# Attention of a fused RWKV-and-experts kernel listed as steps and ordered for every engine by a model, with the 64x64 tiles paired

## The chip, the cores and the metric

One core of a Trainium2 chip. The metric is the device time of one execution in microseconds, the median of the runs shown; a profile is one further execution. TensorE is the matrix engine, VectorE, ScalarE and GpSimd the elementwise engines, SyncE (SP) issues most DMAs.

## The reference

Inputs r, k, v, w, a, b have shape (4, 8, 768, 40): 4 batches, 8 heads, 768 steps, 40 dimensions, float32. Attention is a recurrence over time with a 40x40 state per batch and head; its output, reshaped to 3072 rows of 320, goes through a mixture of 8 experts, one expert per row.

```python
for t in range(S):
    y[:, :, t] = np.einsum('bhd,bhde->bhe', rt, state)
    Sa = np.einsum('bhde,bhe->bhd', state, at)
    state_decay = state * wt[:, :, None, :] - np.einsum('bhd,bhe->bhde', Sa, bt)
    state = state_decay + np.einsum('bhd,bhe->bhde', vt, kt)
...
logits = x @ w_gate
expert_idx = np.argmax(logits, axis=1)
...
h = np.maximum(x_sorted[lo:hi] @ w1[e], 0.0)
y_sorted[lo:hi] = h @ w2[e]
...
return gate_w[:, None] * y
```

## The kernel before

Attention works on 24 units: a unit is one chunk of 64 time steps for two batches, which makes 16 heads in 4 groups p of four. Units alternate between the two pairs of batches (bh), so unit u needs the state of unit u-2. Within a chunk the recurrence becomes products of 64x64 blocks and the inverse of a triangular matrix, taken by repeated squaring (X, X squared and so on) with TT collecting the product of the terms M = 1 + X.

A block takes a quarter of TensorE's 128x128 array: rows 0-63 or 64-127 for the operands, columns 0-63 or 64-127 for the result. `TILES` (L166) walks the four quarters, first the two on the diagonal, then the two that cross. Each fp32 matmul shows in the trace as two matmul and two weight-load records.

- `load(u)` (L196) issues eight DMAs on SP: four of the decays (`dec`, L204) and four of the five other inputs (`in`, L205).
- `prepare(u)` (L207) runs two scans on VectorE (L212, L217), scales K, B and A on GpSimd (L222 to L224), and transposes V, K and B in twelve 128x128 transposes (L230), copied by ScalarE (L235).
- `systems` (L242) forms N (L254), T1 (L267) and G (L284), the product gv (L296), and the inverse: squares (L312), copied by ScalarE (L319, L322), plus one on GpSimd in two halves (`plus_one`, L276), times TT (L329), copied by VectorE (L334).
- `attend` applies the state: ST (L350), r (L354), rhs (L358), u (L363), S (L377), the first part of y (L384), uT (L393), ZT (L407), the new state st (L420, L426) and the rest of y (L440, L448); xT is written at L453. The groups gv, u, S and the first y name the same half for operands and result, so they use the two diagonal quarters only.
- `route` (L458) forms the gate's logits (L466), transposes xT (L470), takes a softmax weight and stores the rows to `x_rows` (L482).

The loop at the end of attention calls load(u+3), prepare(u+2), systems(u+1), attend(u) and route(u); the tile framework orders the instructions from that listing, with `tc.issue_after` (L400, L445) moving two groups behind others. All PSUM results come from one pool of four tiles of two banks (`bank2`, L190). At the start GpSimd clears the padding of the four input buffers in eight halves (L181) and of the other buffers (L184 to L188), and the weights of the first two experts are fetched (`fetch`, L154) ahead of the loop. After attention one core-wide routing step counts and sorts the rows (L507 to L605), and the experts run: gather by indirect DMA (L615), transposes (L625), layer one (L634), layer two (L647), indirect store (L653).

## Time and profile before

| what | us |
|---|---|
| median of 3 runs | 1298.59 |
| runs | 1302.38, 1289.19, 1298.59 |
| the profiled execution's own time | 1284.12 |
| its span, first to last instruction | 1282.4 |
| TensorE matmul busy in the span | 1007.2 (79%), 24316 records |
| TensorE weight loads | 761.6 (59%), 24316 records |
| VectorE, ScalarE, GpSimd | 370.2, 252.2, 406.2 |
| mean granted TensorE clock | 0.896 of full speed |

Busy time is the union of an engine's instructions; matmuls overlap and their ends are modelled, so a busy TensorE is not one at its peak. [...] "Idle before" is the time an engine stood still ahead of an instruction, with what released it behind the arrow; "issue" means that it waited for nothing that the profile shows.

### The profile page before, as it was taken

To read this page: it belongs to the slowest core of one execution; us is meant where nothing else is said; L and a number is where in the kernel's file an instruction comes from. 1 tells how busy PE (TensorE), PEld (TensorE's weight loads), DVE (VectorE), ACT (ScalarE), POOL (GpSimd) and SP (SyncE) were. 2 spreads that over 40 slices of the span, in tenths; PEclk is the share of its full clock that TensorE was granted. 3 is DMA by queue.
4 is the path that set the end of the run, shared out by engine and by line. 5 is a ranking of instruction groups with operands and counts; after the bars stand their busy time and mean duration, and the time that the engine had idled before them with its cause. 6 is when DMAs were issued, how large, how long until landed. Compare 5 with 4: busy or idle time off the path is not lost. (4 is left out here: it accounts for less than half of the span.)

```text
span 1282.4 us, 51696 instructions
## 1 busy us (share of the span) xinstructions
PE 1007.2 (79%) x24316; PEld 761.6 (59%) x24316; DVE 370.2 (29%) x694; ACT 252.2 (20%) x519; POOL 406.2 (32%) x497
## 2 busy tenths in 40 slices
PE   0677777778777777777777877777399999999997
PEld 0566667767666667767666766666235544554444
DVE  0434333333333333333433333331521111011100
ACT  0222222222222222222222222222000011010010
POOL 9643333333333332333333323222332210210011
PEclk9979898887978897887988789889689999999998
DMA  5601112211211121210111111000023322321100
GB/s 155 138 4 44 36 39 40 39 39 22 39 26 34 39 40 39 39 37 19 39 33 33 39 39 35 8 9 9 23 76 109 115 72 74 91 97 52 48 15 16
DMA packets 112682, 61.02 MB, mean 48 GB/s; under 512 B 96849, under 2 KB 108115, under 8 KB 112468
## 3 DMA queue, kind: packets, MB, share of 16 engines
q1 hardware_dynamic: 109056, 48.51, 15.7%
q0 software_dynamic: 3072, 9.18, 2.4%
q8 instruction: 191, 3.13, 1.0%
q14 instruction: 23, 0.19, 0.0%
q10 hardware_dynamic: 340, 0.01, 0.0%
HBM read 49.82 MB, written 9.18 MB: 46 GB/s over the span
## 5 line engine op out<-in xcount | busy, mean ns | idle before, releaser
L276 POOL TENSOR_TENSOR M<-X,ihalf 128x256 f32<-128x256 f32 x240 | 188.7, 809 | 116.9 <-ACT X L322 103.3
L312 PE MATMUL ps_sq<-X 64*64 64x64 f32 x6912 | 175.8, 231 | 35.4 <-ACT X L322 33.1
L634 PE MATMUL hp<-xgT,w 128*128 128x512 f32 (+1 forms) x384 | 192.1, 630 | 0.0
L329 PE MATMUL ps_TT<-TT,M 64*64 64x64 f32 x3840 | 122.8, 240 | 73.1 <-POOL M L276 52.5
L312 PEld LDWEIGHTS ps_sq<-X 64*64 64x64 f32 x6912 | 146.1, 143 | 52.1 <-ACT X L322 47.7
L334 DVE COPY TT<-ps_TT 128x512 f32<-128x512 f32 x120 | 82.9, 691 | 274.5 <-PE ps_TT L329 270.3
L329 PEld LDWEIGHTS ps_TT<-TT,M 64*64 64x64 f32 x3840 | 97.2, 150 | 93.0 <-POOL M L276 89.3
L647 PE MATMUL zp<-w,h_sb 128*128 128x320 f32 x512 | 145.1, 433 | 0.0
L634 PEld LDWEIGHTS hp<-xgT,w 128*128 128x128 f32 (+1 forms) x384 | 63.4, 189 | 123.4 <-issue 122.3
L322 ACT COPY X<-ps_sq 128x512 f32<-128x512 f32 x192 | 103.1, 589 | 141.4 <-PE ps_sq L312 140.1
L224 POOL TENSOR_TENSOR in<-in,q 128x512 f32<-128x512 f32 x24 | 29.3, 1220 | 294.8 <-DVE q L217 294.8
L647 PEld LDWEIGHTS zp<-w,h_sb 128*128 128x128 f32 x512 | 94.6, 191 | 34.5 <-issue 0.8
L639 DVE TENSOR_SCALAR h_sb<-hp 128x512 f32<-128x512 f32 x32 | 22.1, 692 | 247.3 <-PE hp L634 247.3
L653 POOL DMA_INDIRECT out_dram<-zo,s_idx x32 | 31.7, 989 | 181.4 <-ACT zo L652 180.2
L230 PE MATMUL ps_nat<-ident,in 128*128 128x128 f32 x288 | 50.6, 322 | 39.4 <-DMA in<-in_packed_dram 21.2
L276 POOL TENSOR_TENSOR TT<-T,ihalf 128x256 f32<-128x256 f32 x48 | 33.8, 725 | 126.8 <-DVE T L271 126.8
L412 DVE TENSOR_TENSOR ZT<-ps_ZT,m_nn 128x512 f32<-128x512 f32 x24 | 16.6, 691 | 176.0 <-PE ps_ZT L407 176.0
L615 POOL DMA_INDIRECT xg<-x_rows,g_idx x32 | 30.7, 960 | 109.1 <-PE tp L625 78.9
L230 PEld LDWEIGHTS ps_nat<-ident,in 128*128 128x128 f32 x288 | 38.9, 165 | 44.0 <-issue 21.5
L641 ACT ACTIVATE h_sb<-hp 128x512 f32<-128x512 f32 x32 | 19.1, 597 | 198.5 <-PE hp L634 198.5
L296 PE MATMUL ps_gv<-natV,G 64*64 64x40 f32 x768 | 32.3, 229 | 23.3 <-DVE G L289 23.2
L363 PE MATMUL ps_u<-rhs,TT 64*64 64x40 f32 x768 | 36.6, 264 | 17.9 <-DVE rhs L358 17.9
(156 smaller groups left out, 1256.9 us busy)
## 6 DMA issues: line engine op xcount, KB each, us to landing
in<-in_packed_dram SPq DMA_DIRECT2D x96, 200.0 KB
w<-in_moe_w_dram SPq DMA_DIRECT2D x8, 1280.0 KB
w<-in_moe_w_dram SPq DMA_DIRECT2D x8, 1024.0 KB
dec<-in_packed_dram SPq DMA_DIRECT2D x96, 40.0 KB
x_rows<-xs SPq DMA_DIRECT2D x48, 80.0 KB
w<-in_moe_w_dram SPq DMA_DIRECT2D x8, 256.0 KB
xg<-x_rows,g_idx POOLq DMA_INDIRECT x32, 3.0
out_dram<-zo,s_idx POOLq DMA_INDIRECT x32, 2.5
```

Source lines behind the costliest of these rows:

```text
L230: nc.tensor.transpose(ps[:, i % 2, p * 128 : (p + 1) * 128], I[:, n, 2 * p : 2 * p + 2, :].rearrange("x q t -> x (q t)"), ident[:],)
L276: nc.gpsimd.tensor_tensor(dst, src, eye[:, : NP, :], op=ALU.add)
L296: nc.tensor.matmul(gv[halves[q], par, p, :], lhsT=G[halves[q], par, 0, p, :], rhs=Vn[halves[q], p, par, :D], start=True, stop=True,)
L312: nc.tensor.matmul(ps[halves[s], h, w, p, :], lhsT=X[halves[h], s, 1 - w, p, :], rhs=X[halves[h], s, w, p, :], start=True, stop=True,)
L322: nc.scalar.copy(Y[:, s], ps[:, s])
L329: nc.tensor.matmul(ps[halves[s], h, 0, p, :], lhsT=Mk[halves[h], s, p, :], rhs=TT[halves[h], s, p, :], start=True, stop=True,)
L334: nc.vector.tensor_copy(TT[:], ps[:, :, 0])
L363: nc.tensor.matmul(pu[halves[q], par, p, :], lhsT=TT[halves[q], par, p, :], rhs=rhs[halves[q], par, p, :D], start=True, stop=True,)
L615: nc.gpsimd.indirect_dma_start(out=g["xg"][:, j, :], out_offset=None, in_=x_d[:, :], in_offset=bass.IndirectOffsetOnAxis(ap=g["gi"](j), ax ...
L634: nc.tensor.matmul(hp[:, :cols], lhsT=g["w"][0][:dsz, db, fb * 128 : (fb + 1) * 128], rhs=g["xT"][:dsz, db, :cols], start=(db == 0), stop= ...
L647: nc.tensor.matmul(zp[:], lhsT=g["h"][:, fb, j * 128 : (j + 1) * 128], rhs=g["w"][1][:, fb, :], start=(fb == 0), stop=(fb == FB - 1),)
L653: ins_ = nc.gpsimd.indirect_dma_start(out=out[:, :], out_offset=bass.IndirectOffsetOnAxis(ap=g["si"](j), axis=0), in_=zo[:], in_offset=Non ...
```

## The change

Attention is no longer run as functions called unit by unit. `unit(u)` lists steps: each `Step` has an engine, a duration in us (a round of four tiles is `ROUND = 0.116`), a function that emits its instructions, and the buffers that it reads and writes (`Held`). `in_order()` then places all steps of all 24 units by a greedy list: of the steps whose inputs are there in the model, the one that can start earliest on its engine is emitted next, ties by rank (the unit's number, the preparation one unit and the loads three units ahead). Steps marked ANY (PSUM copies) go to ScalarE or VectorE, whichever starts earlier. PSUM is one tile of eight banks, and a step's result gets one or two banks when it is placed. Inside `tc.manual_schedule` every engine runs its instructions in this order.

The layout changes too: N is written crosswise (`halves[1 - q]`), so that TT, gv, u and uT use crossing tiles where they used diagonal ones. gv is interleaved with S, and u with the first part of y. T1's own 16 products are gone; T1 is taken from X by `plus_one` and moved between the halves by four products with `ihalf`, 256 columns wide. GpSimd adds the identity in one instruction instead of two halves, and the last M is added by VectorE. The gate's logits and the transpose of xT are one product with `turn_gate` (the identity beside the negated gate weights). Clearing is shared between GpSimd and VectorE, and the first two experts' weights are fetched in the middle of attention. The experts and the routing step are not touched.

The core of the diff (the functions from `bank2` to the loop over units are removed; only what replaces them is shown):

```diff
-    wg_sb = rte.tile([128, NP, E], F32)
-    nc.gpsimd.memset(wg_sb[:], 0.0)
+    turn_gate = rte.tile([128, NP, 128 + E], F32)
+    nc.gpsimd.memset(turn_gate[:, :, 128:], 0.0)
     for par in range(2):
         nc.scalar.dma_start(
-            wg_sb[par * HP : par * HP + D], moe_w_gate.rearrange("(p a e) n -> a e p n", a=2, e=D)[par],
+            turn_gate[par * HP : par * HP + D, :, 128:], moe_w_gate.rearrange("(p a e) n -> a e p n", a=2, e=D)[par],
         )
+    nc.gpsimd.tensor_scalar(turn_gate[:, :, 128:], turn_gate[:, :, 128:], scalar1=-1.0, scalar2=None, op0=ALU.mult)
+    nc.gpsimd.tensor_copy(turn_gate[:, :, :128], ident[:, None, :].to_broadcast([128, NP, 128]))
...
+    class Step:
+        def __init__(self, rank, eng, cost, fn, reads=(), writes=(), after=(), lag=0.2):
+            self.rank, self.eng, self.cost, self.fn, self.lag = (rank, len(steps)), eng, cost, fn, lag
+            self.deps, self.done, self.next, self.ps = set(after), 0.0, [], []
...
+            steps.append(self)
...
+    def in_order():
+        free = {e: 0.0 for e in (PE, DVE, ACT, POOL, SP)}
+        bank_free = [0.0] * 8
...
+        def place(new, t):
+            ok = [f is not None and f <= t for f in bank_free]
+            at = []
+            for h in new:
+                n = h.banks
+                b = next((b for b in (range(7, -1, -1) if n == 1 else range(7)) if all(ok[b : b + n])), None)
+                if b is None:
+                    return None
+                ok[b : b + n] = [False] * n
+                at.append(b)
+            return at
+        for s in steps:
+            for d in s.deps:
+                d.next.append(s)
+        ready = {s: 0.0 for s in steps if not s.deps}
+        while ready:
+            times = sorted({f for f in bank_free if f is not None})
+            best = None
+            for s, r in ready.items():
+                new = [h for h in s.ps if h.at is None]
+                for e in ((ACT, DVE) if s.eng == ANY else (s.eng,)):
+                    t0 = max(r, free[e])
+                    if best is not None and t0 > best[0][0]:
+                        continue
+                    at = ()
+                    if new:
+                        for t in [t0] + [x for x in times if x > t0]:
+                            at = place(new, t)
+                            if at is not None:
+                                break
+                        else:
+                            continue
+                        t0 = t
+                    cost = s.cost * (1.17 if s.eng == ANY and e == DVE else 1.0)
+                    key = (t0, s.rank, t0 + cost)
+                    if best is None or key < best[0]:
+                        best = (key, s, e, t0, cost, new, at)
+            _, s, e, t, cost, new, at = best
+            del ready[s]
+            for h, b in zip(new, at):
+                h.at = b
+                bank_free[b : b + h.banks] = [None] * h.banks
+            free[e] = t + cost
+            s.done = t + cost + s.lag
+            s.fn(e)
+            for h in s.ps:
+                h.users -= 1
+                if h.users == 0:
+                    for b in range(h.at, h.at + h.banks):
+                        bank_free[b] = s.done
+            for n in s.next:
+                waits[n] -= 1
+                if waits[n] == 0:
+                    ready[n] = max(d.done for d in n.deps)
...
+    ROUND = 0.116
...
+        psum = pp.tile([128, 8, 512], F32, name="ps")
...
+        r_in = Ring("in", [5, SEG, C], 4, 5)
+        r_dec = Ring("dec", [SEG * C1 + 1], 2)
...
+        r_X = Ring("X", [2, 2, NP, C], 5, 2)
+        r_M = Ring("M", [2, NP, C], 3)
+        r_TT = Ring("TT", [2, NP, C], 4)
+        r_G = Ring("G", [2, 2, NP, C], 2, 2)
...
+        for i, (t, held) in enumerate(r_in.bufs):
             for lo in (32, 96):
...
+                zero(-99 + 5 * i, POOL if lo == 32 else DVE, 1.2, t[lo : lo + 32], held)
+        for t, held in r_qini.bufs:
+            zero(-98, POOL, 0.6, t[:], held)
+        for r in (r_rhs, r_ST, r_S):
+            for t, held in r.bufs:
+                zero(-50, POOL, 0.6, t[:], held)
...
+            Step(u - 3, SP, 1.7, lambda e: load(e, 0), writes=hdec, lag=2.5)
+            Step(u - 3, SP, 1.7, lambda e: load(e, 1), writes=hI, lag=3.5)
...
+            def plus_one(x, hx, w):
+                m, hm = r_M.take()
+                Step(u, POOL, 1.25, lambda e: nc.gpsimd.tensor_tensor(m[:], x[:, :, w], eye, op=ALU.add), reads=hx, writes=hm)
+                return m, hm
+            def times(stat, mov, reads, ps):
+                def fn(e):
+                    t = pair(ps, C)
                     for p in range(NP):
                         for h, s in TILES:
...
+                            mm(t[halves[s], h, p, :], stat(h, s, p), mov(h, s, p))
+                Step(u, PE, 4 * ROUND, fn, reads=reads, writes=[ps])
+            def new_TT(ps):
+                t, ht = r_TT.take()
+                Step(u, ANY, 0.59, lambda e: copy(e, t[:], pair(ps, C)), reads=[ps], writes=ht)
+                return t, ht
+            T1, hT1 = plus_one(X, hX, 1)
+            ps = Held(2)
+            def moved(e, ps=ps):
+                t = pair(ps, C)
+                for h, s in TILES:
+                    mm(t[halves[s], h].rearrange("x p j -> x (p j)"), ihalf[halves[h]], T1[halves[h], s].rearrange("x p j -> x (p j)"))
+            Step(u, PE, 4 * ROUND, moved, reads=hT1, writes=[ps])
+            TT, hTT = new_TT(ps)
...
...
+                    Step(u, PE, 8 * ROUND, squares, reads=hX, writes=[ps])
+                    X, hX = r_X.take()
+                    for s in range(2):
+                        Step(u, ANY, 0.59, lambda e, s=s, ps=ps, X=X: copy(e, X[:, s], whole(ps)[:, s]),
+                             reads=[ps], writes=hX[s : s + 1])
+                    M, hM = plus_one(X, hX, 0)
+                else:
+                    times(lambda h, s, p, X=X: X[halves[h], s, 1, p, :], lambda h, s, p, X=X: X[halves[h], s, 0, p, :], hX, ps)
+                    M, hM = r_M.take()
+                    Step(u, DVE, 0.69, lambda e, ps=ps, M=M: nc.vector.tensor_tensor(M[:], pair(ps, C), eye, op=ALU.add),
+                         reads=[ps], writes=hM)
+                ps = Held(2)
+                times(lambda h, s, p, M=M: M[halves[h], s, p, :], lambda h, s, p, TT=TT: TT[halves[h], s, p, :], hM + hTT, ps)
+                TT, hTT = new_TT(ps)
...
+            def p_gv(e):
+                for p in range(NP):
+                    for i in range(2):
+                        for q in range(2):
+                            par = q ^ i
+                            mm(single(psg)[halves[1 - q], par, p, :], G[halves[q], par, 0, p, :], nV[halves[q], p, par, :D])
+                        if c:
+                            for par in range(2):
+                                mm(single(psS)[halves[par], i, p, :], ST[halves[par], i, p, :], ihalf[halves[par], :D])
+            Step(u, PE, 8 * ROUND, p_gv, reads=hG + hnV + (hST if c else []), writes=[psg] + ([psS] if c else []))
...
+            def p_u(e):
+                t = single(psu)
+                for p in range(NP):
+                    for i in range(2):
+                        for q in range(2):
+                            par = q ^ i
+                            mm(t[halves[q], par, p, :], TT[halves[1 - q], par, p, :], rhs[halves[1 - q], par, p, :D])
+                        if c:
+                            for par in range(2):
+                                mm(
+                                    pair(psy, C)[halves[par], i, p, :], Sn[halves[par], i, p, :], head(R, p, i, par),
+                                    start=(p == 0), stop=False,
+                                )
+            s_u = Step(u, PE, 8 * ROUND, p_u, reads=hTT + hrhs + (hSn + [hI[R]] if c else []), writes=[psu] + ([psy] if c else []))
...
+            Step(u, PE, 4 * ROUND, p_uT, reads=hTT + hrhs, writes=[ps], after=[s_u])
...
+            late = u + 1
+            s_ = bh * NCH + c
+            psx = Held(2)
+            WX = 128 + E
+            def p_x(e):
                 for p in range(NP):
...
+                    mm(psum[:, psx.at + p // 2, p % 2 * WX : (p % 2 + 1) * WX], xT[:, p].rearrange("x q j -> x (q j)"), turn_gate[:, p, :])
+            Step(late, PE, 0.95, p_x, reads=hxT, writes=[psx])
...
+        for u in range(NU):
+            unit(u)
+        def first_weights(e):
+            for i in range(2):
+                weights[i] = fetch(moe_w1[i], moe_w2[i])
+        Step(8, SP, 2.0, first_weights, after=[s for s in steps if s.eng == SP][-3 * (NU - 12) - 1 :][:1])
+        with tc.manual_schedule(engines={getattr(mybir.EngineType, n) for n in ENGINES}):
+            in_order()
```

## Rows read from the trace of the kernel before

**Rows 1.** Busy time by stage: columns length, busy time (instructions) per engine, granted clock, DMA share, GB/s.
```profile
44.00:905.00 861.00, 654.25 (x23271) 587.73 (x23271) 302.00 (x512) 214.42 (x446) 297.76 (x354) 0.87 0.16 33
905.00:1282.00 377.00, 346.80 (x1024) 169.39 (x1022) 61.33 (x176) 33.62 (x67) 67.66 (x68) 0.95 0.21 67
```

**Rows 2.** Line L453 on VectorE, the write of xT: all 24, and the last but one.
```profile
L453 DVE TENSOR_TENSOR xT<-ps_y,q x24: 690/691/692, 98.5 to 903.1; 128x512 f32<-128x512 f32 x24
...
889.21 0.69 DVE L453 TENSOR_TENSOR xT<-ps_y,q 128x512 f32<-128x512 f32 x1 [1.28 <-PE ps_y L448]
```

**Rows 3.** Groups by line: busy us, mean ns; idle before and its releasers.
```profile
L276 POOL TENSOR_TENSOR M<-X,ihalf 128x256 f32<-128x256 f32 x240 | 188.7, 809 | 116.9 <-ACT X L322 103.3 <-ACT X L319 13.4
...
L329 PE MATMUL ps_TT<-TT,M 64*64 64x64 f32 x3840 | 122.8, 240 | 73.1 <-POOL M L276 52.5 <-DVE TT L334 18.6 <-issue 0.8
L322 ACT COPY X<-ps_sq 128x512 f32<-128x512 f32 x192 | 103.1, 589 | 141.4 <-PE ps_sq L312 140.1 <-POOL M L276 1.3
...
L334 DVE COPY TT<-ps_TT 128x512 f32<-128x512 f32 x120 | 82.9, 691 | 274.5 <-PE ps_TT L329 270.3 <-POOL M L276 4.3
...
L212 DVE TENSOR_TENSOR_SCAN rv<-dec,ones 128x521 f32<-128x521 f32 x24 | 38.6, 1609 | 33.0 <-DMA dec<-in_packed_dram 32.4 <-DMA in<-in_packed_dram 0.6
...
L222 POOL TENSOR_TENSOR in<-in,rv 128x512 f32<-128x512 f32 x24 | 29.3, 1220 | 0.8 <-DVE rv L212 0.8
```

**Rows 4.** Timeline of TensorE, 450 to 459 us and at 757.75: start, length, records.
```profile
451.21 1.13 PE L363 MATMUL ps_u<-rhs,TT 64*64 64x40 f32 x32 [0.85 <-DVE rhs L358]
452.14 1.18 PE L377 MATMUL ps_S<-ihalf,ST 64*64 64x40 f32 x32
...
456.68 0.63 PE L420 MATMUL ps_st<-natV,natK 64*64 64x40 f32 x32
457.12 0.66 PE L426 MATMUL ps_st<-U,natB 64*64 64x40 f32 x32
...
757.75 0.66 PE L230 MATMUL ps_nat<-ident,in 128*128 128x128 f32 x4
```

**Rows 5.** DMA queues of the page: packets, MB, share of 16 engines.
```profile
q8 instruction: 191, 3.13, 1.0%
```

**Rows 6.** Timeline of TensorE, 818.7 to 822.6 us, the first and the last of six rows.
```profile
818.79 0.33 PE L407 MATMUL ps_ZT<-in,uT 64*64 64x64 f32 x9
...
822.18 0.34 PE L448 MATMUL ps_y<-G,natK 64*64 64x64 f32 x8 [1.20 <-issue]
```

**Rows 7.** Timeline of TensorE, 872 to 877 us, the rows after two stalls.
```profile
872.52 0.50 PE L312 MATMUL ps_sq<-X 64*64 64x64 f32 x18 [0.15 <-issue]
...
876.22 0.50 PE L329 MATMUL ps_TT<-TT,M 64*64 64x64 f32 x18 [0.46 <-issue]
```

**Rows 8.** Slices of 0.2 us, columns as in rows 1.
```profile
819.40:819.60 0.20, 0.20 (x28) 0.20 (x22) 0.20 (x1) 0.00 (x0) 0.00 (x0) 1.00 0.37 82
870.00:870.20 0.20, 0.20 (x30) 0.20 (x21) 0.00 (x0) 0.00 (x0) 0.00 (x0) 1.00 0.29 82
873.60:873.80 0.20, 0.03 (x1) 0.03 (x1) 0.20 (x1) 0.20 (x2) 0.00 (x0) 1.00 0.38 82
```

**Rows 9.** TensorE after two stalls while inputs load, and a slice between them.
```profile
761.22 0.35 PE L284 MATMUL ps_G<-in 64*64 64x64 f32 x8 [0.21 <-issue]
...
767.24 1.44 PE L312 MATMUL ps_sq<-X 64*64 64x64 f32 x42 [0.33 <-issue]
...
763.50:764.00 0.50, 0.50 (x34) 0.50 (x32) 0.00 (x0) 0.00 (x0) 0.00 (x0) 1.00 0.87 116
```

**Rows 10.** The start: the first 32 us by engine, GpSimd's clears, the first scan, the first N.
```profile
0.00:32.00 32.00, 1.09 (x4) 0.71 (x4) 0.00 (x0) 1.87 (x2) 30.28 (x68) 1.00 0.58 155
...
14.73 11.27 POOL L181 MEMSET in<- 32x2560 f32 x5
...
32.35 1.24 DVE L212 TENSOR_TENSOR_SCAN rv<-dec,ones 128x521 f32<-128x521 f32 x1 [32.35 <-DMA dec<-in_packed_dram]
...
44.14 1.99 PE L254 MATMUL ps_N<-in 64*64 64x64 f32 x64
```

## Prediction

> **What bounds the kernel now.** I read the page's busy shares first, then busy time by stage, the groups of instructions, one unit's timeline, and last the DMA traffic in slices of 0.2 us. The stages [rows 1]: attention runs from 44 to 905 us (861 us for 24 units), routing and experts from 905 to 1282, which the diff leaves alone. In attention TensorE is busy 654 of 861 us at a mean granted clock of 0.87, VectorE 302, GpSimd 298, ScalarE 214: no engine is full. The output step ends at 98.5 us for the first unit and 903.1 us for the last [rows 2], 35 us apart on average. Inside a unit the engines hand one chain back and forth: TensorE's products for TT waited 73 us, mostly for GpSimd's M, GpSimd 103 us for ScalarE's X, ScalarE 140 us for TensorE's squares, VectorE 270 us for TT's products [rows 3]. So the order binds first: the systems of unit u+1 run almost alone, then attend(u) almost alone. That is what the change goes after.

> **Pairing.** Four groups of 16 matmuls (u, S, the first y, gv) use only the two diagonal tiles. From L363's start to L377's: 0.93 us for 32 records (16 fp32 matmuls, two records each); the products of L420, on all four tiles, take 0.44 [rows 4]. Paired, gv with S and u with the first y, each group loses 0.49 us: 4 x 0.49 x 24 = 47 us of TensorE time, on the path as long as TensorE sets the pace. T1's 16 products give way to 4 wide ones with ihalf (256 columns each, four times a usual one's; an estimate, 0.46 us in place of 0.46, so nothing).

> **Order.** If it does what it lists, the fullest engine sets the pace. TensorE per unit: 464 ordinary matmuls are 116 rounds of four, the wide ones 4 more; a round is 0.44/4 = 0.11 to 0.116 us, 13.8 us. 12 transposes at 0.66 us per four at most [rows 4] are 1.65 to 2.0; the gate products, four where there were twelve instructions, 0.5 to 1.4, I take 0.95. Sum 16.5 us. VectorE and ScalarE: some 25 PSUM reads of 512 columns at 0.69 or 0.59 us, two scans of up to 1.6 [rows 3], and some 5 us (an estimate by size) of six reads of 320 columns and of small ones: 24 us over two engines, 12 each. GpSimd: three multiplies at 1.22 and five additions of 512 columns, bounded by one and two of today's halves (0.81 to 1.62 [rows 3]), nearer to the multiply of the same size: 3.7 + 5 x 1.4 = 10.7. A bank pair is held from its first matmul to its last read, 1.4 to 4 us, psy 6: some 90 bank-us per unit, 11.5 us over 8 banks. All lie under TensorE's 16.5, which lies under today's 35. By engines alone a unit could come at 17.7 (with drains between tile modes) to 20 us.

> [...]

> After the change a unit has 468 matmuls x 2 + 8 + 12 = 956 records and as many weight loads, against 984: 24 units less the first and last chunks' savings make 22,624 x 2 / 256 = 176.8 blocks. So 176.8 x 3.7 = 654 us is the least, however good the order. Loads delay a fetch: at 767.24 a block came 6.0 us after the stall at 761.22, with the DMA engines 0.87 busy at 763.5 us in between [rows 9]. Loads keep them so for about 6.5 us of each unit; I charge one or two blocks of 7.4 with 1 to 2 us more, 0.3 us on the mean, and bound it by 0 and 2.3. Where the granted clock falls to half, a block's 16 rounds need 3.7 us themselves and only waits add. I take 4.0 us a block, between 3.6 and 4.4: 707 us, 29.5 per unit. In that state the pairing's 47 us and most of the order's gain lie under the fetch; they are worth something only down to this floor.

> **Start, weights, tail.** Today the two experts' weights go first on SP, the first scan waits for dec until 32.35 us, GpSimd clears input buffers, eight halves at 2.25 us, until 26 us, and the first N product starts at 44.14 [rows 10]; the DMA moved 155 GB/s meanwhile. The change defers the weights and gives half the clearing to VectorE: GpSimd has 26 - 8 x 2.25 = 8 us of constants, then four halves, 9 us, some 4 us of smaller clears (an estimate by size) and two multiplies, 2.4: N at 23 to 28 us, I take 25; at worst 44. The 5.1 MB of weights then lie inside attention: 33 us at 155 GB/s, in which blocks take 6.0 instead of 4.0: 10 us (0 to 15). Behind the fetch on SP's queue wait the next units' loads, which have two units' lead and hide. The last unit has nobody to fill its waits: today the last attend takes 13.9 us alone, from one xT to the next [rows 2]; I add 12 (5 to 20).

> **The sum.** Attention's end: 25 + 707 + 10 + 12 = 754 us, against 905: 151 less. The profiled execution took 1284.1 us (span 1282.4), so 1133 us. The runs shown have a median of 1298.6, 1.1% above that execution; I keep 1133.

> **Rivals.**
> (a) The supply does not bind: the stalls are chance, or fetches run further ahead in a dense stream. For it: only 8 us of stalls today. Against it: blocks average 4.74 us today, so a deeper store would always be full, yet it ran dry after one block. Then units at 19 us: 25 + 456 + 12 = 493, 412 less: 872 us.
> (b) The order does not hold: each engine's list is fixed, and where a duration is off (GpSimd beside VectorE's scans, a cold clock), the engine stands at its head with ready work behind. For it: the durations in the list are constants, and it has 1.25 us for an addition whose two halves take 1.62 today [rows 3]. Against it: waits then must cover all the slack between 16.5 and 30 us. A block every 4.5 us: 796 + 47 = 843, 62 less: 1222 us.
> (c) Slower: fetches collide with loads all the time, since a faster PE also asks for loads sooner, and every block takes 6.0 us as at 767.24: 1061 + 47 = 1108, 203 more: 1487 us. It decides from (905 - 47)/176.8 = 4.85 us per block. Against it: a unit's loads fill only 6.5 us of its time, and no faster than units end.

> **How the numbers follow.** Forecast 0.72, (a) 0.14, (b) 0.09, (c) 0.05. The forecast's own range, 3.6 to 4.4 us per block with the start and tail bounds, is 1055 to 1205. I give 1045 to 1210: it leaves out (a), most of (c) and the far part of (b). A difference of about 1% is what a measurement of this kernel can tell from none; faster by more than that 0.94 (forecast, (a), most of (b)), within it 0.02, slower 0.04.

> **What would show it.** Right: attention ends near 754 us; no engine is full, TensorE about 55 to 65% busy there; its idle time stands under "issue", not under semaphores, in stalls of 1 to 2 us about every 254 instructions; single 16.4 KB bursts come every 3.6 to 4.0 us where nothing else is loaded; the diagonal groups' 0.93 us are gone; N starts at about 25 us. Wrong: units at 17 to 20 us with blocks under 2.5 us (a); TensorE waiting mostly for ScalarE, VectorE or GpSimd (b); blocks over 4.85 us (c).

## The result, and the profile after

The changed kernel takes 1103.14 us (median of 4 runs, 1101.03 to 1109.93) against 1297.48 for the kernel before (a fourth run of it took 1296.37): a ratio of 0.852 (95% interval 0.846 to 0.858), 194 us less. The forecast was 1133, with a range of 1045 to 1210. The profiled execution took 1102.44 us with a span of 1100.7. Medians and ratios below leave out slow runs, those over 1.5% above the fastest of the same kernel: one of the first merge (1076.04 us) and two of the kernel before.

The page of the changed kernel, busy times, clock, and the DMA queue that carries instructions:

```profile
PE 837.7 (76%) x23644; PEld 614.6 (56%) x23644; DVE 400.8 (36%) x769; ACT 247.5 (22%) x504; POOL 340.1 (31%) x318
...
PEclk9999899899989979998999899957999999999998
...
q8 instruction: 186, 3.05, 1.2%
```

The write of xT, which ends attention (it answers to [rows 2]), and busy time by stage (to [rows 1]; the columns are length, busy time of TensorE, weight loads, VectorE, ScalarE and GpSimd with their instructions, granted clock, DMA share, GB/s):

```profile
L637 DVE TENSOR_TENSOR xT<-ps,q x24: 680/692/693, 76.0 to 716.6; 128x512 f32<-128x512 f32 x24
```

```profile
30.40:390.00 359.60, 253.42 (x11937) 230.76 (x11937) 174.17 (x307) 114.90 (x235) 140.18 (x106) 0.95 0.23 45
390.00:411.00 21.00, 13.12 (x459) 11.43 (x461) 7.04 (x13) 3.12 (x6) 1.27 (x1) 0.76 1.01 272
411.00:685.00 274.00, 195.76 (x9171) 177.91 (x9170) 130.21 (x233) 82.41 (x172) 98.75 (x75) 0.94 0.19 38
685.00:716.60 31.60, 21.99 (x1056) 19.62 (x1046) 10.48 (x20) 9.90 (x20) 5.07 (x4) 0.98 0.04 10
716.00:1100.70 384.70, 349.08 (x1052) 171.36 (x1044) 62.73 (x178) 33.54 (x67) 67.77 (x68) 0.94 0.22 66
```

All of the gain lies in attention: the last xT comes at 716.6 us instead of 903.1, 186.5 earlier, 28 us apart on the mean instead of 35. What follows is 4.8 us longer (384.1 after 379.3 us, from the last xT to the end of the span).

Is TensorE's time the limit now? No: it is busy in 484 of attention's 686 us. The groups by line and the waits on TensorE say what it does in the rest:

```profile
L358 PE MATMUL ps<-X 64*64 64x64 f32 x6912 | 148.1, 228 | 68.3 <-issue 67.0 <-ACT TT L353 1.2
...
L358 PE MATMUL ps<-TT,M 64*64 64x64 f32 x3840 | 94.9, 228 | 37.2 <-issue 36.7
```

```profile
PE ps L358 <- issue: 193.7, 149, 4.5
...
PE ps L358 <- ACT TT L353: 2.4, 6, 0.7
PE ps L358 <- DVE ZT L621: 0.9, 1, 0.9
```

Before, the products for TT stood idle 73 us, most of it for GpSimd's M and VectorE's TT [rows 3]. Now they stand idle 37 us, nearly all of it for nothing that the profile names. So do all of TensorE's products: 194 us in 149 stalls (the columns of the waits are us in total, times, longest). The timeline of TensorE shows where these stalls are. Start, length, records, and in brackets the idle time before; all rows between the first two stalls, and the rows at the next two:

```profile
43.31 0.28 PE L358 MATMUL ps<-TT,M 64*64 64x64 f32 x4 [2.07 <-issue]
43.41 0.22 PE L358 MATMUL ps<-X 64*64 64x64 f32 x1
43.42 0.23 PE L358 MATMUL ps<-TT,M 64*64 64x64 f32 x3
43.47 1.11 PE L358 MATMUL ps<-X 64*64 64x64 f32 x63
44.51 0.66 PE L411 MATMUL ps<-ident,in 128*128 128x128 f32 x4
45.10 1.03 PE L358 MATMUL ps<-X 64*64 64x64 f32 x52
47.19 0.39 PE L358 MATMUL ps<-X 64*64 64x64 f32 x11 [1.06 <-issue]
...
50.75 0.37 PE L358 MATMUL ps<-natV,G 64*64 64x40 f32 x6 [1.14 <-issue]
...
54.57 0.45 PE L358 MATMUL ps<-X 64*64 64x64 f32 x13 [1.63 <-issue]
```

Count the records between the first two brackets: 4 + 1 + 3 + 63 + 4 + 52 = 127, with as many weight loads 254 instructions. The next stall comes 128 records on, the next 127. The line of the program and the kind of product don't matter; the count does. This is the block of about 256 instructions that [rows 6, 7] showed now and then (the first bare section below has 128 records to the block, 256 instructions with their weight loads), and here most blocks end so: counted over all records of attention, there are 141 stalls of over 0.3 us under "issue" for some 176 blocks, and each lies a whole number of blocks behind the one before, to within two records: one block 113 times, two 21 times, three 6 times. A single block takes 3.80 us in the median (3.45 at the least), whereas the products between 43.31 and 47.19 keep TensorE busy for under 3.

And where nothing else is loaded, slices of 0.2 us show the block's transfer itself, as in [rows 8]:

```profile
644.80:645.00 0.20, 0.20 (x29) 0.20 (x24) 0.04 (x1) 0.00 (x0) 0.00 (x0) 1.00 0.33 82
648.40:648.60 0.20, 0.20 (x21) 0.18 (x13) 0.20 (x1) 0.20 (x1) 0.00 (x0) 1.00 0.30 82
652.20:652.40 0.20, 0.20 (x27) 0.20 (x23) 0.00 (x0) 0.00 (x0) 0.00 (x0) 1.00 0.30 82
655.80:656.00 0.20, 0.20 (x10) 0.15 (x3) 0.00 (x0) 0.03 (x1) 0.20 (x1) 1.00 0.43 82
```

One burst every 3.6 to 3.8 us, 16.4 KB each (82 GB/s over 0.2 us). The packets of the instruction queue, taken one by one from the trace, tie burst and stall together: in each of the 113 single blocks exactly one packet of 16,384 bytes starts, 1.17 us after the block was entered in the median (1.04 to 5.49), and TensorE goes on 2.16 to 2.89 us after that start. So where a block comes late, it is mostly because its packet started late.

### The profile page after: what moved, and what is told of

Its sections match the earlier page's. It is cut to its first block, busy times and chain, and to the rows that moved or that the text cites. A ratio compares the mean times of both kernels' runs of the same rounds, so it can differ in the third digit from the quotient of the medians.

```text
span 1100.7 us, 50357 instructions
## 1 busy us (share of the span) xinstructions
PE 837.7 (76%) x23644; PEld 614.6 (56%) x23644; DVE 400.8 (36%) x769; ACT 247.5 (22%) x504; POOL 340.1 (31%) x318
## 5 line engine op out<-in xcount | busy, mean ns | idle before, releaser
L442 POOL TENSOR_TENSOR M<-X,ihalf 128x512 f32<-128x512 f32 x120 | 165.0, 1378 | 349.3 <-DVE X L355 194.0
L358 PE MATMUL ps<-X 64*64 64x64 f32 x6912 | 148.1, 228 | 68.3 <-issue 67.0
L358 PEld LDWEIGHTS ps<-X 64*64 64x64 f32 x6912 | 131.1, 142 | 79.2 <-issue 75.7
L358 PE MATMUL ps<-TT,M 64*64 64x64 f32 x3840 | 94.9, 228 | 37.2 <-issue 36.7
L353 ACT COPY TT<-ps 128x512 f32<-128x512 f32 x122 | 71.6, 587 | 193.5 <-PE ps L358 187.0
L358 PEld LDWEIGHTS ps<-TT,M 64*64 64x64 f32 x3840 | 79.5, 141 | 45.2 <-issue 43.2
L353 ACT COPY X<-ps 128x512 f32<-128x512 f32 x109 | 62.8, 587 | 172.0 <-PE ps L358 170.0
L355 DVE COPY X<-ps 128x512 f32<-128x512 f32 x83 | 57.3, 690 | 107.6 <-PE ps L358 106.2
L358 PE MATMUL ps<-in 64*64 64x64 f32 x3072 | 61.6, 223 | 23.8 <-issue 23.5
L401 POOL TENSOR_TENSOR in<-in,rv 128x512 f32<-128x512 f32 x48 | 60.8, 1276 | 47.5 <-DMA in<-in_packed_dram 39.6
```

The costliest lines, as they stand in the source:

```text
L353: nc.scalar.copy(dst, src)
L355: nc.vector.tensor_copy(dst, src)
L358: nc.tensor.matmul(out_, lhsT=lhsT, rhs=rhs, start=start, stop=stop, skip_group_check=True)
L401: Step(pre, POOL, 1.22, lambda e, n=n, by=by: nc.gpsimd.tensor_tensor(I[:, n], I[:, n], by, op=ALU.mult), reads=hb, writes=hI[n : n + 1])
L442: Step(u, POOL, 1.25, lambda e: nc.gpsimd.tensor_tensor(m[:], x[:, :, w], eye, op=ALU.add), reads=hx, writes=hm)
```

## The experiments

The theory: attention's pace is TensorE's supply of instructions, some 3.8 us per 256 of them, whatever they do. The rivals: the products' own time on the tiles sets it; the chain from engine to engine sets it; the stalls are something else that happens to show as "issue". Medians are compared with the changed kernel's 1103.14 us, ratios with the kernel before, which was run beside each set of experiments (medians of 1291 to 1299 us); the intervals are some 0.7% to either side, so a difference of under 8 us says little by itself.

### Pairing undone

```diff
                             mm(single(psg)[halves[1 - q], par, p, :], G[halves[q], par, 0, p, :], nV[halves[q], p, par, :D])
+                for p in range(NP):
+                    for i in range(2):
                         if c:
...
                             mm(t[halves[q], par, p, :], TT[halves[1 - q], par, p, :], rhs[halves[1 - q], par, p, :D])
+                for p in range(NP):
+                    for i in range(2):
                         if c:
```

> The changed kernel with the pairing undone: gv's 16 products come before S's 16, u's before y's, so two tiles run at a time where four did; the instructions are the same in number. Instruction supply (176.8 blocks of 256, 3.8 us each): the longer steps lie inside the stalls, within 1% of the changed kernel, 0 to +10 us. TensorE's tile time: two steps of 0.93 us more per unit, 24 units, +45 us. Waits on other engines: between the two.

Measured: 1104.1 us (1103.1 to 1113.37), ratio 0.859 (0.851 to 0.867). The last xT comes at 719.8 us, 3 later. The pairing is worth nothing that can be told from the noise. Two rows of this run say why, the page's busy time and TensorE's wait:

```profile
PE 859.8 (78%) x23644; PEld 639.1 (58%) x23644; DVE 402.3 (37%) x769; ACT 248.1 (23%) x504; POOL 339.2 (31%) x318
```

```profile
PE ps L358 <- issue: 172.7, 135, 4.1
```

TensorE works 22 us longer than with the pairs (859.8 against 837.7), and its unnamed stalls are 21 us shorter (172.7 against 193.7). Work put into a block is taken out of the stall at its end. A theory of tile time can't give that: by it the 22 us would be added to the whole.

### Fewer instructions: two merges, apart and together

The first merge forms the new state and y in the same products, 104 columns wide instead of 40 and 64; the second forms the squares and the products for TT of three levels together, 128 columns wide, with four wide identity products per level; it also spares GpSimd three additions per unit, for which TensorE shows no wait in the changed kernel. Both keep the computation and, but for the identities, the columns.

```diff
+            def p_two(e, stat, mov, first):
+                for p in range(NP):
+                    for q, par in TILES:
+                        mm(both()[halves[par], q, p, :WY], stat[halves[q], p, par, :],
+                           mov[halves[q], p, par, :], start=(c == 0 and first and p == 0), stop=(not first))
...
-            Step(u, PE, 4 * ROUND, lambda e: p_y(e, 0, nB, lambda p, q, par: ZT[halves[q], par, p, :]),
-                 reads=hnB + hZT, writes=[psy])
-            Step(u, PE, 4 * ROUND, lambda e: p_y(e, 1, nK, lambda p, q, par: G[halves[q], par, 1, p, :]),
-                 reads=hnK + hG, writes=[psy])
+            Step(u, PE, 6.5 * ROUND, lambda e: p_two(e, nB, ZU, True), reads=hnB + hZU, writes=[psy])
+            Step(u, PE, 6.5 * ROUND, lambda e: p_two(e, nK, GV, False), reads=hnK + hGV, writes=[psy])
...
+                    for p in range(NP):
+                        for h, s in TILES:
+                            mm(t[halves[s], h, :, p, :], X[halves[h], s, 0, p, :], X[halves[h], s, 1:3, p, :], start=(p == 0), stop=False)
+                    for h, s in TILES:
+                        mm(t[halves[s], h, 1].rearrange("x p j -> x (p j)"), ihalf[halves[h]],
+                           X[halves[h], s, 2].rearrange("x p j -> x (p j)"), start=False)
```

The first alone:

> The changed kernel with the state's update and y's two products, which have the same stationary tile, issued as one product of 104 columns (40 + 64) instead of two. 32 matmuls fewer per unit in 22 of 24 units, 2816 instructions or 11 blocks fewer, the streamed columns nearly the same. Instruction supply: 11 x 3.8 = 42 us less than the changed kernel (30 to 50). Tile time: no change (under 5 us). Waits: no change or slower, since the state now waits for ZT as well.

The second alone:

> Only the second half of the merged version: the squares and the products for TT of three levels share their moving operand's columns (128 instead of 64), with 4 wide identity products per level. Per unit 144 instructions of TensorE fewer, 24 x 144 / 256 = 13.5 blocks. Supply theory: 13.5 x 3.77 = -51 us against the changed kernel, -35 to -60. Theory that TensorE's time at its tiles sets the pace: no columns are saved and some wide products added, 0 to +33 us. Theory that the chain of engines sets the pace: one PSUM read more per level, 0 to +20 us.

Both:

> As e2_merged, and three levels of the inverse have the second square and the product for TT, both with X as the stationary tile, issued as one product of 128 columns, with TT itself added by four wide products by the identity. 144 instructions fewer per unit on top, together 24.5 blocks fewer; TensorE streams 3 x 0.46 us more per unit. Instruction supply: 24.5 x 3.8 = 93 us less than the changed kernel, near 1010 us (990 to 1030). Tile time: 33 us more, 1136. Waits: GpSimd has three additions less per unit, which would help if it were waited for; up to 20 us less.

| kernel | records x 2 fewer, in blocks | us | against 1103.14 | ratio to before |
|---|---|---|---|---|
| first merge | 11.0 | 1065.39 | -38 | 0.830 (0.822 to 0.838) |
| second merge | 13.5 | 1052.21 | -51 | 0.807 (0.800 to 0.813) |
| both | 24.5 | 1017.78 | -85 | 0.792 (0.785 to 0.798) |

The blocks are the page's matmul records: (23644 - 22236) x 2 / 256 = 11.0, (23644 - 21916) x 2 / 256 = 13.5, (23644 - 20508) x 2 / 256 = 24.5. The gain per block is 3.4, 3.8 and 3.5 us, and the two merges add up, all to within the 8 us of noise on each time. By the ratios the gains are 28, 58 and 78 us, and by the last xT (672.7, 669.2 and 631.3 us) 44, 47 and 85. The instruction queue and TensorE's wait of the run with both:

```profile
PE 834.1 (82%) x20508; PEld 602.1 (59%) x20508; DVE 392.6 (39%) x773; ACT 243.1 (24%) x500; POOL 243.4 (24%) x246
...
q8 instruction: 161, 2.64, 1.1%
```

```profile
PE ps L360 <- issue: 100.3, 96, 5.5
```

25 packets fewer than 186 are 25 blocks, as counted. TensorE's busy time is all but unchanged (834.1 against 837.7); what is gone is stall: 100 us are left of 194. This version beats both kernels. The rival of the engines' chain allowed no gain for either merge alone and up to 20 us for both; 38, 51 and 85 were measured.

### What the supply gives by itself

Bare products on 64x64 tiles, five sections of them:

```diff
+            for h, s in TILES:
+                nc.tensor.matmul(
+                    ps[halves[s], h, :cols], lhsT=S[halves[h], i % 8, :], rhs=M[halves[h], :cols],
+                    start=True, stop=True, skip_group_check=True,
+                )
```

> This kernel leaves out the whole computation but for five bare sections of fp32 products on 64x64 tiles, with constants as operands: 640 of 64 columns, 640 of 16, 640 of 128, 320 of 256, then 640 of 64 while input loads run. A product is 4 instructions (two weight loads, two matmuls), so 64 products are one block of 256 instructions. Supply theory: 3.5 to 3.8 us per block for 64 and for 16 columns alike (35 to 38 us per section), about the same for 128 (whose own tile time is 3.7), 6.8 to 7 for 256, where the products themselves last longer than a fetch, and more than the first section for the last, beside the loads. Theory that tile time sets the pace: 1.86 us per block for 64 columns (19 us per section), at most 1 for 16, 3.7 for 128, 6.8 for 256, and no difference with loads.

The timeline of TensorE, the first section (64 columns) and the first rows of the second (16), then the fourth (256) and the last (64, beside loads):

```profile
1.99 7.38 PE L52 MATMUL a<-M,S 64*64 64x64 f32 x351 [1.99 <-DVE M L42]
10.74 2.09 PE L52 MATMUL a<-M,S 64*64 64x64 f32 x128 [1.36 <-issue]
14.46 2.09 PE L52 MATMUL a<-M,S 64*64 64x64 f32 x128 [1.64 <-issue]
18.19 2.09 PE L52 MATMUL a<-M,S 64*64 64x64 f32 x128 [1.64 <-issue]
...
36.29 0.70 PE L52 MATMUL a<-M,S 64*64 64x64 f32 x33 [1.64 <-issue]
36.80 1.53 PE L52 MATMUL b<-M,S 64*64 64x16 f32 x95
40.01 11.06 PE L52 MATMUL b<-M,S 64*64 64x16 f32 x384 [1.68 <-issue]
...
111.78 34.74 PE L52 MATMUL d<-M,S 64*64 64x256 f32 x640
...
158.77 2.09 PE L52 MATMUL e<-M,S 64*64 64x64 f32 x128 [1.91 <-issue]
162.78 2.09 PE L52 MATMUL e<-M,S 64*64 64x64 f32 x128 [1.91 <-issue]
167.33 2.09 PE L52 MATMUL e<-M,S 64*64 64x64 f32 x128 [2.46 <-issue]
```

The first section settles it without a wait for any other engine, without a semaphore or an order: 128 records exactly, 2.09 us long, then 1.36 or 1.64 us of nothing. From 10.74 to 36.29 seven blocks take 25.55 us, 3.65 each. The 256-column section takes 34.74 us for five blocks, 6.95 each, with no stall, as the products' own time says. Two sections don't decide: the one of 128 columns, at 3.8 us a block (37.9 us for ten, from 73.9 us), comes out the same by both theories, and in the one of 16 columns the granted clock was 0.50, at which the records lie end to end and a block takes 3.7 us too:

```profile
10.74:36.29 25.55, 14.64 (x898) 13.70 (x897) 0.00 (x0) 5.17 (x3) 1.00 0.49 100
40.00:73.00 33.00, 31.99 (x1152) 31.36 (x1152) 0.00 (x0) 0.00 (x0) 0.50 0.02 4
151.04:182.24 31.20, 16.73 (x1024) 15.66 (x1024) 0.00 (x0) 0.00 (x0) 1.00 0.36 68
```

(Columns here: length, TensorE, weight loads, VectorE, GpSimd, clock, DMA share, GB/s.) The block ahead of those at 0.50, 33 records of 64 columns and 95 of 16, still ran at a clock of 0.95 to 1.00: it took 3.72 us, 1.68 of them stall, as the supply has it. The expectation of at most 1 us for a block of 16 columns fails by its products alone: 95 records took 1.53 us, each as long as with 64 columns. Nor do these sections settle what loads cost: the last is slower, 31.20 / 8 = 3.90 us a block, but part of the loads ran beside the first section already, at 100 GB/s, and there the blocks stayed at 3.65.

### What input loads cost the fetches

```diff
                             nc.sync.dma_start(dst5[rows(par), q], src[:, 1:])
+                            nc.sync.dma_start(extra[u % 2, q, par], src[:, 1:])
```

> The changed kernel with each of the four large input loads of a unit issued a second time into a scratch tensor that nothing reads: 0.8 MB more traffic per unit, no other change. Instruction supply: fetches of blocks wait behind more load traffic; two to three blocks of 7.4 instead of one or two come late by 1 to 2 us, +15 to +60 us. Tile time or waits on engines: the loads have two units' lead, so no change, under 6 us.

Measured: 1127.49 us (1122.19 to 1129.72), 24 more, ratio 0.876 (0.869 to 0.882). Inside the stated range, but not for the stated reason alone: the first N came at 42.5 us instead of 30.4, since the second copies also stand in the way of the first unit's inputs. So I ran it again with the copies from the fourth unit on (`if u >= 3`):

> As the run with every large input load issued twice, but the second copies start with the fourth unit, so that the start is the changed kernel's: first N at 30 us. It asks what loads cost the fetches by themselves. If the +24 us of that run were late fetches: +20 or more again, with blocks at about 3.95 us on the mean. If half of it was the start (its first N came at 42.5 us instead of 30.4) and the loads cost the fetches little: +5 to +12, blocks at 3.88 to 3.92 instead of 3.84.

Measured: 1116.23 us (1114.11 to 1118.56), 13 more, ratio 0.862 (0.858 to 0.866), one above the +5 to +12 that went with half of it being the start; the first N at 31.8, so about half was the start indeed. Two stages of this run, columns as in the table by stage above:

```profile
30.40:390.00 359.60, 247.18 (x11720) 224.94 (x11720) 169.51 (x296) 110.35 (x225) 134.27 (x103) 0.96 0.33 74
...
430.00:700.00 270.00, 188.77 (x8928) 171.68 (x8932) 126.57 (x225) 79.20 (x164) 92.35 (x72) 0.94 0.26 57
```

Blocks are records x 2 / 256: 359.6 / 91.6 = 3.93 us each, or 3.91 counted from the first N at 31.8, where the changed kernel has 359.6 / 93.3 = 3.86, and later 270 / 69.75 = 3.87 against 274 / 71.65 = 3.82. Doubling the loads costs a block 0.05 to 0.06 us, some 10 us over attention; the rest of the 13 probably lies where the experts' weights come in as well (a stall of 5.49 us there is the longest of the run).

### The weights first again

```diff
-        Step(8, SP, 2.0, first_weights, after=[s for s in steps if s.eng == SP][-3 * (NU - 12) - 1 :][:1])
+        Step(-200, SP, 2.0, first_weights)
```

> The first two experts' weights (5.1 MB) are issued first on SP again, as before the change; nothing else is touched. Supply theory with the terms of the trace: the weights' transfers lengthened two blocks inside attention (7.96 and 7.57 us instead of 3.77), so taking them out of attention gives back about 8 us; ahead of the first unit's loads they hold back the first scan, so that the first N comes at about 44 us as before instead of 30.4, 14 us later. Sum +6 us, 0 to +12. If the start costs nothing (the first N stays at 30): -8 us. If the weights were hidden in attention: +14 us.

Measured: 1109.07 us (1104.93 to 1116.6), 6 more, ratio 0.853 (0.846 to 0.860): too little to tell from nothing by the times. The trace shows both terms, each smaller than expected: the first N at 42.0 us (11.6 later, not 14), the last xT at 723.7, so attention itself lasts 681.7 instead of 686.2 us (4.5 less, not 8). Moving the weights into attention gains 11.6 us at the start and costs 4.5 of them again.

### The order undone

The same steps, pairs and banks, but every engine takes its steps by rank, unit by unit.

```diff
-                    if best is not None and t0 > best[0][0]:
+                    if best is not None and s.rank > best[0][0]:
...
-                    key = (t0, s.rank, t0 + cost)
+                    key = (s.rank, t0, t0 + cost)
```

> The order is undone, the rest of the change is kept: the same steps with the same pairing and the same giving out of banks, but each engine takes them by their rank, unit by unit, instead of by the earliest start that the model gives. If the order is what filled the waits: TensorE waits for X, M and TT again, its idle time stands under the other engines and not under issue, and the attention part goes back towards 35 us a unit: 1250 us or more. If the gain came from the supply, the pairing or the start alone: no more than 50 us above the changed kernel.

Measured: 1532.57 us (one run), 429 more, and more than the kernel before. The groups by line, the waits, and attention as one stage (columns as in the table by stage above):

```profile
L358 PE MATMUL ps<-X 64*64 64x64 f32 x6912 | 188.9, 286 | 0.9 <-issue 0.9
...
L358 PE MATMUL ps<-TT,M 64*64 64x64 f32 x3840 | 118.4, 286 | 244.4 <-POOL M L442 220.3 <-DVE M L489 24.1
```

```profile
PE ps L358 <- POOL M L442: 287.3, 120, 2.8
...
PE ps L358 <- POOL in L401: 102.3, 24, 23.8
```

```profile
62.40:1148.30 1085.90, 603.12 (x21764) 543.88 (x21764) 319.13 (x547) 219.57 (x437) 225.45 (x184) 0.70 0.14 30
```

The unnamed stalls of the squares are gone (0.9 us instead of 67.0), and in their place TensorE waits 287 us for M and 102 for the next unit's inputs. By the rows of xT (62.4 to 1148.3 us) a unit takes 47 us, which makes 6.4 us a block, and the fetch is hidden. Part of the loss is probably the clock: it is 0.70 on the mean here, and TensorE is busy 603 us where the changed kernel has 484. So the change needs its order to come down to the floor of the supply; pairs and banks alone don't get there. Whether the order would do so with the old layout and banks, no run shows. The kernel before stands between the two, probably because its listing lets two units overlap and its M comes in halves [rows 3]; that is not tested.

## Why the prediction was right

**The limit was named rightly.** The step on which all rests (one block is fetched while one runs, and the next takes about 3.7 us whatever the block does) was read from two stretches of the kernel before [rows 6 to 8]; the merges (11, 13.5 and 24.5 blocks fewer, 3.4 to 3.8 us each) and the bare products (128 records between stalls) show it as cause. Rival (a), units at 17 to 20 us, falls: no two stalls stand closer than 3.45 us a block. Rival (b), the order does not hold, falls by TensorE's waits: beside 193.7 us of "issue", attention's products waited 2.4 us for ScalarE's TT, 0.9 for VectorE's ZT, and less for anything else; TensorE's longest waits for another engine or a load in attention's part lie ahead of the first N (below). Rival (c), every block at 6.0 us, falls: blocks of over 5 us are a handful of single ones (5.94 us at 321.38, 7.96 and 7.57 beside the weights). What a wrong order would cost is shown all the same by the run above: 1532 us, dearer than (b) or (c) put it.

**The reading behind it** was weaker than it looked. Of the two stretches only the second is a count. In the first, the 129 records from 818.79 us start where the view starts: no stall stands there, and the row of 9 is the end of 32 records that began at 818.43 behind a wait for ScalarE's uT. The 3.7 us rest on one interval, and that it lay so near the median of 3.80 was luck, since single blocks with no weights beside them take 3.45 to 5.94. A packet's "some 270" instructions counted those of all engines; TensorE's alone make 24,316 x 2 / 191 = 255.

**The terms.** Attention ended at 716.6 us, not at 754: 37 less, in four terms.

| term | predicted | measured | by which rows |
|---|---|---|---|
| first N | 25 | 30.4 | the first start of the N products |
| blocks | 176.8 x 4.0 = 707 | 176.8 x 3.84 = 679 | 359.6 us / 93.3 and 274 / 71.65 blocks |
| weights | 10 | 7 | 390 to 411: 21 us for 3.6 blocks, 3.85 each |
| tail | 12 | 0 | 685 to 716.6: 31.6 us for 8.25 blocks, 3.83 each |

30.4 + 679 + 7 = 716. The largest miss is the charge for loads, 0.3 us on every block: it was taken from a single block of 6.0 us [rows 9]. The doubled loads put it at 0.05 to 0.06. Between the bare products' 3.65 and attention's 3.86 lies mostly a later start of the packets: in the single blocks from 30.4 to 390 us a packet starts 1.33 us after the block was entered on the mean, in the first bare section 1.11, while the time from its start to the next instruction is the same (2.57 and 2.54). What delays the start stays open; with the loads doubled it is 1.35. In the stretch with next to no loads (685 to 716.6) the six single blocks take 3.59 us each, and its mean of 3.83 holds waits at the end of the last chain as well.

Two more numbers were off without harm. TensorE was busy 484 of 686 us, 71% and not 55 to 65%: 20.2 us a unit where the forecast's sum had 16.5, which only shortened the stalls. And the range of 1055 to 1205 is not what its bounds add up to: N at 23 to 28, weights 0 to 15, tail 5 to 20 and 3.6 to 4.4 us a block give 1044 to 1220.

Three things that the forecast named without a measurement stand in the trace of the kernel before, read from the starts and lengths of the records. What it called drains between tile modes: the first 64x64 record starts 203 ns behind the last 128x128 one (46 times, in the median), where two transposes start 110 ns apart. A granted clock of half: from the first start to the last, the 32 records of L420 take 401 ns where the clock was 1.0 and 733 where it was 0.5. GpSimd beside VectorE's scans: an addition of M (L276) takes 713 to 732 ns where no scan runs, and 1619 to 1747 in the 22 cases in which a scan runs beside it for over 1 us.

**The tail** was thought to be a unit without company, at the pace of today's last attend [rows 2]. But the last two chains together still gave TensorE more than the supply let through; only behind 710 us does it wait for ScalarE and VectorE, 0.7 to 0.9 us each.

**The start.** N came 5 us later than forecast, within the bound of 44. GpSimd's clears ended at 21.4 us, as the forecast had it (8 + 9 + 4), and the multiply by q, the last that N needs, at 24.84, where the forecast had 25. But on TensorE N stands behind five groups of four transposes, and the last of these waited for a load that landed at 29.4 us. The copy behind it is the third of natV, so this is V of a third unit, which the list, going by its own durations, had put ahead of the first unit's N. That is rival (b) in small; the forecast had looked at GpSimd alone.

```profile
22.62 2.82 PE L411 MATMUL ps<-ident,in 128*128 128x128 f32 x12 [4.13 <-POOL in L401]
29.36 1.08 PE L411 MATMUL ps<-ident,in 128*128 128x128 f32 x4 [3.91 <-DMA in<-in_packed_dram]
30.37 2.97 PE L358 MATMUL ps<-in 64*64 64x64 f32 x128
...
23.67 1.17 POOL L401 TENSOR_TENSOR in<-in,q 128x512 f32<-128x512 f32 x1
...
30.48 0.59 ACT L353 COPY natV<-ps 128x512 f32<-128x512 f32 x1 [4.41 <-PE ps L411]
```

**Pairing** was said to be worth 47 us of TensorE's time and to vanish under the fetch. It did vanish; its size was 22 us (the page's busy times, 859.8 against 837.7), probably because the unpaired groups overlap with their neighbours more than the time from L363's start to L377's had shown [rows 4]; no run takes that apart.

**What follows attention** was taken as unchanged, and is 4.8 us longer. On VectorE the routing's first score follows the last xT by 7.4 us (716.63 to 724.03), where the kernel before has 2.9 (903.13 to 906.03 in its timeline of VectorE): it now stands behind the last rows' gate, and its wait of 2.81 us ends with the store of those rows.

```profile
720.84 0.38 DVE L676 TENSOR_SCALAR xs<-ps,g 128x160 f32<-128x160 f32 x1
724.03 0.36 DVE L700 TENSOR_TENSOR sc<-lgn,lmin 128x192 f32<-128x192 f32 x1 [2.81 <-DMA x_rows<-xs]
```

**The sum.** 716.6 + 384.1 + 1.7 around the span is 1102.4, against 754 + 377 + 1.7. So 31 us too high: 37 in attention, less 7 behind it, 4.8 for the routing and 2 for taking the end of attention at 905 us instead of at the last xT.

## What to carry to other kernels

When an engine stands still for nothing that the profile names, count the instructions between two such stalls: if the count is the same each time, or a multiple of it (here 126 to 128 records a block, 252 to 256 instructions), the instructions themselves are late. Then a change that packs the same instructions closer (a better order, pairing tiles) is worth something only down to that floor (here a median of 3.80 us a block; undoing the pairs cost 1 us), and one that does the same columns with fewer instructions goes below it (here by 38, 51 and 85 us). A stall that shows in a few places of a slow kernel can give the floor of a faster one (here 3.7 us from one interval); a cost per block should be taken from many blocks, not from the worst one.

## What the runs showed of the hardware that I had not expected

- The fetch of a block is steadier than one row had made me think. In the first section of bare products stalls come 3.45 or 3.73 us apart and nothing else, with the DMA engines 0.49 busy on the mean; in attention it is 3.82 to 3.91 us on the mean at DMA shares of 0.19 to 0.33. Only the weights' transfer, with a DMA share of 1.01, hurt much: 21.0 / 3.6 = 5.8 us a block. There two packets started 5.49 and 4.91 us after their block was entered, and yet TensorE went on 2.46 and 2.66 us later, as ever.
- The bare kernel started with 351 records in one piece, 702 instructions or 2.7 blocks, and in that section ran dry after every single block of 128 records from there, for 1.36 or 1.64 us. Why the first piece was longer, no run shows.
- The more a block has to do, the less of it is stall, to about a microsecond: undoing the pairs took 21 us from "issue", added 22 to "busy" (76 to 78% of the span) and left the time where it was (1104.1 against 1103.14 us). A busy share that rises is no gain, and one that falls no loss, while the supply sets the pace.
